# Pooled attention and feed-forward: two engines' queues in written order from chunk 3 on, attention in half-tile steps, and weight sums built in other buffers

## The chip, the cores and the metric

The kernel runs on one core of one Trainium2 chip. The metric is the device time of one execution in microseconds (us). TensorE (PE) multiplies, VectorE (DVE) and ScalarE (ACT) work on tiles in SBUF and PSUM, GpSimd (POOL) on tiles in SBUF alone, and SyncE (SP) issues most DMAs; a few DMAs are issued by ACT.

## The reference

```python
# q, k, v: [8 batches, 8 heads, 576, 64]; w_in: [512, 2048]; w_out: [2048, 512]; all float32
k_p = k.reshape(B, H, 72, 8, 64).mean(axis=3)          # keys and values pooled by 8
v_p = v.reshape(B, H, 72, 8, 64).mean(axis=3)
scores = q @ k_p.T / 8; scores -= max(scores)
attn = exp(scores); attn /= sum(attn) + 1e-9
x = heads_side_by_side(attn @ v_p)                       # 4608 tokens x 512
h = x @ w_in
out = maximum(0.01 * h, h) @ w_out                       # 4608 x 512
```

## The kernel before

The 4608 tokens are cut into nine chunks of 512, numbered 0 to 8. For each chunk the feed-forward multiplies on PE in split float32 (a high part and a low part of each operand), and beside it, in the same stretch of time, the attention of the next chunk's tokens is computed: `runs` lists the stretches, `beside` the attention pieces that go with each, and a stretch takes its attention steps one by one as its matmuls go by. The name of a chunk stands in its tiles' names: the tile B113xh is operand B11 of chunk 3, B116xh that of chunk 6. Chunks 3 to 8 use a scheme with seven products per quarter-block instead of eight (`pair`, `combine`, PE line 1080); it needs sums of weight blocks, which `prepare(j)` builds once for each of eight pairs of weight columns and ships to DRAM (`kept`), from where ACT's queue streams them in again for every chunk.

Batches 2 to 7 go through a path that transposes in DRAM. One half of a tile (four heads) takes these steps. PE computes scores (`s`, line 549), DVE the maximum, ACT four exponentials (559), DVE the reciprocal and POOL the normalised rows (`sb`, lines 593 and 599). SP writes them to DRAM (`rows`, line 606) and reads them back in another order (`blocks`, line 616). DVE transposes blocks of 32 (`pp`, line 628), ACT casts them to pT_hi (651), DVE makes pT_lo and the remainder (654, 658), all of which is the step `pu`. PE multiplies with the values (`au`, lines 673 to 676) and ACT copies the result into the next chunk's x (689). Keys and values of a batch are loaded by SP and summed by 8 on POOL in `lk` and `lv` (lines 264 and 271): k in two halves, its remainder, v in two halves, its remainder. The eight DMAs of v's remainder are at line 317. They all go through the pool tag `raw`, which has two buffers; tiles of the weight sums, and output tiles of one stretch (line 1212), have the same tag. `ku` places the keys (435, 440), and `vu` the values: v_hi on ACT (463), v_lo on DVE (466), v_parts on ACT (472), then four operations on DVE.

The order within an engine's queue comes from two sources. PE's instructions stand in written order (`manual_schedule`). On every other engine a planner orders them by a simulated timeline and by priorities, except for those marked with `keep_in_program_order`, which stay in written order among themselves. Each engine then runs its queue strictly in that order, so an instruction that waits holds up all behind it.

Of the kernel before, what the change touches and what calls it, by code (L numbers as in the profile page):

```python
# [24 lines left out]
def tile_pooled_attention_ffn(  # L25
# [52 lines left out]
    SUMS = ["S1", "S2", "S3", "S4", "A22"]  # L78
# [249 lines left out]
    def load_k(b):  # L328
        sums = one.tile([P, NK, D], F32, tag="ksum", name=f"ksum{b}") if b > 1 else addup[:, 7:]
        rem = k_rem  # L330
        if b < 2:
            rem = addup[:, 3 + 2 * b : 5 + 2 * b, :].unsqueeze(1)
        eng = nc.vector if b == 0 else nc.gpsimd
        raws = []

        def start():
            raws.extend(load_main(b, k, g, "k") for g in range(2))
            raws.append(load_k_rem(b))

# [22 lines left out]
        return start, finish  # L362

    def load_v(b):
# [25 lines left out]
        return start, finish  # L390

    tiles = [[x for piece in p for x in piece] for p in PIECES]
    every = [(b, t) for b in range(B) for t in range(len(tiles[b]))]

# [20 lines left out]
    def place_k(b, sums, rem):  # L415
# [11 lines left out]
        else:  # L427

            for i in range(2):
                for c in range(2):  # L430
                    to = slice(64 * i + 32 * c, 64 * i + 32 * c + 32)
                    cols = slice(32 * c, 32 * c + 32)
                    for x in range(2):
                        r = slice(64 * i + 32 * x, 64 * i + 32 * x + 32)
                        nc.vector.transpose(  # L435
                            kT[to, :, i, 32 * x : 32 * x + 32], sums[r, :, cols]
                        )
                    for x in range(2):
                        r = slice(32 * x, 32 * x + 32)
                        nc.vector.transpose(  # L440
                            kT[to, 2 * x : 2 * x + 2, :, MAIN:], rem[r, 0, i, cols]
                        )
# [7 lines left out]
    def place_v(b, sums, rem):  # L450
# [10 lines left out]
        for i in range(2):  # L461
            r = slice(64 * i, 64 * i + 64)
            nc.scalar.mul(v_hi[r, :, i, :], sums[r], 1.0 / POOL)
        for i in range(2):
            r = slice(64 * i, 64 * i + 64)
            nc.vector.scalar_tensor_tensor(
                v_lo[r, :, i, :], sums[r], 1.0 / POOL, v_hi[r, :, i, :].bitcast(F32),
                op0=ALU.mult, op1=ALU.subtract,
            )
        if b > 1:  # L470

            nc.scalar.mul(v_parts, rem, 1.0 / POOL)
            nc.vector.scalar_tensor_tensor(
                rem, rem, 1.0 / POOL, v_parts.bitcast(F32), op0=ALU.mult, op1=ALU.subtract
            )
# [31 lines left out]
    def q_unit(b, t, qr):  # L507
        n = tiles[b][t][1]
        if b > 1:
# [4 lines left out]
            nc.vector.transpose(  # L514
                qT[:, :, :n].rearrange("k p (s g) -> k g p s", g=m),
                blocks.rearrange("a (g p d) -> a g p d", g=m, p=NK),
            )
# [68 lines left out]
    def norm_via(b, t, g, e, sm):  # L586
# [16 lines left out]
        )  # L603
        rows = dram.tile([4, n, 96], F32, name=f"rows{b}_{t}_{g}")
        with tc.high_priority():
            nc.sync.dma_start(
                rows.rearrange("x a y -> a x y"), at[:n].rearrange("a x i j -> a x (i j)")
            )
        return rows

    def fetch_via(b, t, g, rows):

        m = tiles[b][t][1] // 32
        blocks = three.tile([P, 4, 3, 32], F32, tag="at", name=f"blocks{b}_{t}_{g}")
        with tc.high_priority():
            nc.sync.dma_start(
                blocks[:, :m].rearrange("p a i j -> p (a i j)"),
                rows.rearrange("x (s a) y -> (x s) (a y)", a=m),
            )
        return blocks  # L620

    def turn_via(b, t, g, blocks):
# [4 lines left out]
        tc.keep_in_program_order(  # L627
            nc.vector.transpose(  # L628
                pp[:, :, :n].rearrange("k i (s a) -> k a i s", a=m), blocks[:, :m]
            )  # L630
        )
# [137 lines left out]
    def attention(b):  # L769
# [5 lines left out]
        def loads():  # L775
            (start_k, st["k"]), (start_v, st["v"]) = load_k(b), load_v(b)
# [7 lines left out]
        def loads1():  # L784
            (start_k, st["k"]), (start_v, st["v"]) = load_k(b), load_v(b)
# [9 lines left out]
        def ku():  # L795
            place_k(b, *st["ks"])

        def vu():
            place_v(b, *st["vs"])

        def qu(t):
            def f():
                st["qT", t] = q_unit(b, t, q_of[b, t])
                after = every.index((b, t)) + 2
                if after < len(every) and every[after] not in q_of:
                    q_of[every[after]] = load_q(*every[after])
            return f

# [11 lines left out]
        def sb(t, g):  # L820
            def f():
                norm = norm_via if b >= VIA else norm_unit
                st["at", t, g] = norm(b, t, g, *st["e", t, g])
            return f

        def fe(t, g):
            def f():
                st["at", t, g] = fetch_via(b, t, g, st["at", t, g])
            return f

        def pu(t, g):
            def f():
                j, o = where[t]
                if (j, g) not in st:
                    st[j, g] = piece_tiles(b, j, g)
                p_unit(b, t, g, st["at", t, g], st[j, g], o)
            return f

        def au(j, g):
# [5 lines left out]
            "loads": loads1 if b else loads, "lk": lk, "lv": lv, "ku": ku, "vu": vu,  # L845
            **{f"q{t}": qu(t) for t in range(len(where))},
            **{f"s{t}": both(sa(t, 0), sa(t, 1)) for t in range(len(where))},
            **{f"{n}{t}{g}": u(t, g) for n, u in (("sa", sa), ("sb", sb), ("fe", fe), ("pu", pu))
# [61 lines left out]
    def line_up_via(pieces):  # L910

        flat = [(b, j, t) for b, j in pieces for t in range(len(tiles[b]))
                if tiles[b][t] in PIECES[b][j]]
        out, ends, free = [], {}, 0
# [20 lines left out]
        for n, (b, j, t) in enumerate(flat):  # L935
            nxt = flat[n + 1] if n + 1 < len(flat) else None
            if t == 0:
                out.append((b, "ku"))
            if n == 0:
                out.append((b, f"q{t}"))  # L940
            if nxt is None or nxt[:2] != (b, j):
                slots = stages(b, j, [x[2] for x in flat if x[:2] == (b, j)])
                if nxt and nxt[0] != b:
                    slots[-1].append((nxt[0], "vu"))
# [5 lines left out]
            for g in range(2):  # L950

                out.append(None if g else (b, f"s{t}"))
                if g == 0 and nxt:
                    out.append((nxt[0], f"q{nxt[2]}"))
                out.append((b, f"sb{t}{g}"))
                if g == 1 and n == 0 and t == 0:
                    out.append((b, "vu"))
                out += ends.pop(2 * n + g, [])
        for key in sorted(ends):
            out += [None, *ends[key]]  # L960
# [57 lines left out]

    kept = dram.tile([len(PAIRS), P, len(SUMS), 2, HALF], F32, name="kept")

    def prepare(j):

        ship = []
        f0, f1 = PAIRS[j]
        w = two.tile([P, 2, DM], F32, tag="raw", name=f"wsum{j}")
        for i, f in enumerate((f0, f1)):
            whole = ws[0, f].bitcast(F32)
            nc.gpsimd.tensor_tensor(w[:, i, :], whole[:, 0, :], whole[:, 1, :], op=ALU.add)
        (a11, a12), (a21, a22) = ((w[:, i, :HALF], w[:, i, HALF:]) for i in range(2))
# [4 lines left out]
        for i, names in enumerate((("S2", "S4"), ("S3", "S1"))):  # L1034
            both = two.tile([P, 2, DM], F32R, tag="raw", name=f"wsumhl{j}{i}")
            h, l = both[:, 0, :], both[:, 1, :]
            nc.scalar.copy(h, w[:, i, :])
            nc.gpsimd.tensor_tensor(l, w[:, i, :], h.bitcast(F32), op=ALU.subtract)
            for x, name in enumerate(names):
                ship.append((name, both.bitcast(F32)[:, :, x * HALF : (x + 1) * HALF]))  # L1040
        if j < OPEN:
            ship.append(("A22", ws[0, f1].bitcast(F32)[:, :, HALF:]))

        def send():
            for name, of in ship:
                tc.keep_in_program_order(nc.sync.dma_start(kept[j, :, SUMS.index(name)], of))
# [17 lines left out]
    def stream(eng, j, name):  # L1064

        if name == "S3":
            to, of = seat(name).bitcast(F32), kept[j, :, 2]
        else:
            seat(name)
            f, i, m = (2, 0, 2) if name == "S1" else (3, 3, 2 if j < OPEN else 1)  # L1070
# [212 lines left out]
    units = []  # L1283
    for n, pieces in enumerate(beside):
# [3 lines left out]
            for x in line_up_via([x for x in pieces if x[0] >= VIA])  # L1288
# [99 lines left out]
    going = list(range(len(PAIRS)))  # L1388
    for n in range(REST + FAST - 1, len(runs)):
# [4 lines left out]
        if nxt:  # L1394
            if nxt in waiting:
                us.insert(0, lambda nxt=nxt: carry(nxt))
            mid = len(us) // 2
            for b in early[n]:
                us[mid:mid] = [att[b]["lk"], att[b]["lv"]]
        beat = done = 0  # L1400
        for i, j in enumerate(going):
            final = i == len(going) - 1
            send()
            send = prepare(PREPARE[n, i]) if (n, i) in PREPARE else lambda: None
# [46 lines left out]
```

## Time and profile before

| what | value |
|---|---|
| three timed runs | 1007.02, 1004.08 and 1006.77 us, median 1006.77 us |
| profiled execution, its own time | 1004.5 us |
| its span, first to last instruction | 1002.7 us |
| mean granted TensorE clock | 0.959 of full speed |
| busy share of the span: PE, DVE, ACT, POOL | 90%, 53%, 48%, 30% |

The profiled execution's own time is the one that sums are made against; 1.8 us of it lie outside the span. A busy PE is not yet a PE at full speed, since it is counted as busy at half its clock too. The two levels of the clock are 2.4 and 1.2 GHz, so a granted clock of 0.94 over a stretch means that 12% of it ran at half speed.

### The profile page before, as it was taken

To read this page: it belongs to the slowest core of one execution; us is meant where nothing else is said; L and a number is where in the kernel's file an instruction comes from. 1 tells how busy PE (TensorE), PEld (TensorE's weight loads), DVE (VectorE), ACT (ScalarE), POOL (GpSimd) and SP (SyncE) were. 2 spreads that over 40 slices of the span, in tenths; PEclk is the share of its full clock that TensorE was granted. 3 is DMA by queue.
4 is the path that set the end of the run, shared out by engine and by line. 5 is a ranking of instruction groups with operands and counts; after the bars stand their busy time and mean duration, and the time that the engine had idled before them with its cause. 6 is when DMAs were issued, how large, how long until landed. Compare 5 with 4: busy or idle time off the path is not lost.

```text
span 1002.7 us, 15139 instructions
## 1 busy us (share of the span) xinstructions
PE 906.0 (90%) x5163; PEld 789.8 (79%) x5163; DVE 529.6 (53%) x1170; ACT 479.6 (48%) x1474; POOL 304.0 (30%) x470
## 2 busy tenths in 40 slices
PE   4689999979799779997899969997999899999998
PEld 4578898857688668886788858886988799988987
DVE  6998577543265444563555545654655453334212
ACT  6787576352254344453555425553555355344332
POOL 4501201735355764444333033411321022001000
PEclk9799999989799979999899979998999999999999
DMA  9963303354347513896178635863376316423432
GB/s 273 305 192 123 85 23 89 92 168 118 107 130 216 137 64 90 255 235 166 42 198 214 183 85 140 212 162 103 81 186 170 112 54 187 144 85 106 114 108 93
DMA packets 168717, 141.51 MB, mean 141 GB/s; under 512 B 101184, under 2 KB 141888, under 8 KB 168640
## 3 DMA queue, kind: packets, MB, share of 16 engines
q1 hardware_dynamic: 144976, 90.86, 33.2%
q10 hardware_dynamic: 23664, 49.68, 17.1%
q8 instruction: 41, 0.67, 0.3%
q14 instruction: 36, 0.29, 0.1%
HBM read 109.97 MB, written 30.54 MB: 140 GB/s over the span
## 4 chain that ended last, share of the span: by engine, by line
PE 38%; DMA 7%; DVE 4%; ACT 2%; POOL 2%; SPq 2%; issue 1%; ACTq 0%; POOLq 0%; DVEq 0%
PE ends_y L1080 10%; PE ends_x L1080 7%; PE acc L1174 6%; PE acc L1175 6%; PE acc L1176 6%; DMA vremraw<-in_v_dram 2%; PE pss L549 1%; DMA blocks<-rows 1%; DMA out_dram<-o 1%; DVE pp L628 1%; DVE kT L435 1%; PE pa L674 1%; DMA kremraw<-in_k_dram 1%; POOL vremraw L264 1%; PE pa L673 1%
## 5 line engine op out<-in xcount | busy, mean ns | idle before, releaser
L1174 PE MATMUL acc<-w,gh 128*128 128x512 f32 x576 | 232.1, 403 | 8.5 <-DVE o L1213 6.7
L1175 PE MATMUL acc<-w,gh 128*128 128x512 f32 x576 | 228.4, 397 | 0.0
L1176 PE MATMUL acc<-w,gl 128*128 128x512 f32 x576 | 226.6, 393 | 0.5 <-DVE gl L1111 0.5
L1174 PEld LDWEIGHTS acc<-w,gh 128*128 128x128 f32 x576 | 110.3, 192 | 25.5 <-issue 9.9
L1176 PEld LDWEIGHTS acc<-w,gl 128*128 128x128 f32 x576 | 109.4, 190 | 25.7 <-DVE gl L1111 0.9
L1175 PEld LDWEIGHTS acc<-w,gh 128*128 128x128 f32 x576 | 110.3, 191 | 14.0
L559 ACT ACTIVATE e<-pss,red 128x72 f32<-128x72 f32 (+1 forms) x320 | 97.9, 327 | 39.3 <-DVE red L557 36.6
L593 POOL TENSOR_TENSOR at<-e,red 128x128 f32<-128x128 f32 (+1 forms) x120 | 48.3, 422 | 149.0 <-DVE red L590 71.6
L992 PE MATMUL ph<-xh,w 128*128 128x512 f32 (+1 forms) x224 | 85.2, 380 | 0.4 <-DVE gl L1001 0.4
L993 PE MATMUL ph<-xl,w 128*128 128x512 f32 (+1 forms) x224 | 82.6, 369 | 0.0
L994 PE MATMUL ph<-xh,w 128*128 128x512 f32 (+1 forms) x224 | 82.5, 368 | 0.0
L673 PE MATMUL pa<-pT_hi,v_hi 128*128 128x256 f32 (+2 forms) x72 | 25.4, 353 | 47.6 <-ACT pT_hi L651 47.0
L559 ACT ACTIVATION_READ_ACCUMULATOR e<-pss,red 128x1 f32 (+1 forms) x320 | 68.1, 213 | 0.0
L651 ACT CAST pT_hi<-pp 128x384 fp32r<-128x384 f32 (+1 forms) x80 | 37.7, 474 | 49.8 <-DVE pp L628 46.2
L654 DVE TENSOR_TENSOR pT_lo<-pp,pT_hi 128x256 fp32r<-128x256 f32 (+1 forms) x80 | 38.2, 477 | 43.5 <-ACT pT_hi L651 43.2
L1001 DVE TENSOR_TENSOR gl<-ph,gh 128x512 fp32r<-128x512 f32 (+1 forms) x56 | 34.1, 610 | 48.3 <-ACT gh L1000 47.9
L1111 DVE TENSOR_TENSOR gl<-off,gh 128x512 fp32r<-128x512 f32 x48 | 34.2, 712 | 46.7 <-ACT gh L1110 46.2
L673 PEld LDWEIGHTS pa<-pT_hi,v_hi 128*128 128x128 f32 x72 | 15.8, 220 | 54.5 <-ACT pT_hi L651 52.7
L1139 ACT ACTIVATE dia<-dia 128x256 f32<-128x256 f32 x48 | 20.1, 419 | 74.8 <-DVE dia L1138 74.8
L1131 ACT ACTIVATE dia<-ends_x 128x256 f32<-128x256 f32 x48 | 18.6, 387 | 75.0 <-PE ends_x L1080 75.0
L628 DVE STREAM_TRANSPOSE pp<-blocks 128x384 f32<-128x384 f32 (+1 forms) x60 | 45.8, 763 | 16.2 <-DMA blocks<-rows 16.2
L1130 DVE TENSOR_TENSOR ends_y<-ends_y,dia 128x256 f32<-128x256 f32 x48 | 20.8, 434 | 60.3 <-PE ends_y L1080 60.2
(428 smaller groups left out, 2249.0 us busy)
## 6 DMA issues: line engine op xcount, KB each, us to landing
seat<-kept ACTq DMA_DIRECT2D x63, 512.0 KB
w<-kept ACTq DMA_DIRECT2D x42, 256.0 KB
rows<-at SPq DMA_DIRECT2D x48, 192.0 KB
blocks<-rows SPq DMA_DIRECT2D x48, 192.0 KB
out_dram<-o SPq DMA_DIRECT2D x34, 256.0 KB
w_bits<-in_moe_w_in_dram SPq DMA_DIRECT2D x16, 512.0 KB
w_bits<-in_moe_w_out_dram SPq DMA_DIRECT2D x16, 512.0 KB
kept<-wsumhl SPq DMA_DIRECT2D x32, 256.0 KB
```

The source lines that it names most:

```text
L559: ins = nc.scalar.activation(e[:n, h, :], scv[:n, h, :], AF.Exp, bias=mx[:n, h : h + 1], accum_out=sm[:n, h : h + 1],)
L593: nc.gpsimd.tensor_tensor(at[:n, :, i, :].rearrange("a (h f) j -> a h f j", h=2), e[:n, 2 * i : 2 * i + 2, 0:MAIN].rearrange("a h (f j) -> ...
L628: nc.vector.transpose(pp[:, :, :n].rearrange("k i (s a) -> k a i s", a=m), blocks[:, :m])
L654: nc.vector.tensor_tensor(pc["lo"][:, :, o : o + n], pp[:, 0:2, :n], pc["hi"][:, 0:2, o : o + n].bitcast(F32), op=ALU.subtract,)
L673: nc.tensor.matmul(pa, vh, pc["hi"][:, i, :w], start=True, stop=False)
L992: nc.tensor.matmul(ph, w[:, 0, ks], xh[kk][:, r], start=kk == 0, stop=False)
L993: nc.tensor.matmul(ph, w[:, 0, ks], xl[kk][:, r], start=False, stop=False)
L994: nc.tensor.matmul(ph, w[:, 1, ks], xh[kk][:, r], start=False, stop=kk == NK - 1)
L1080: nc.tensor.matmul(out, w[:, stay, ks], move, start=start and i + n == 0, stop=i + n == 3, skip_group_check=True,)
L1174: nc.tensor.matmul(a, gh[:, r], hi, start=first, stop=False)
L1175: nc.tensor.matmul(a, gh[:, r], lo, start=False, stop=False)
L1176: nc.tensor.matmul(a, gl[:, r], hi, start=False, stop=last)
```

## The change

- From the stretch of chunk 3 on, POOL's and SP's queues stand in written order as PE's does (`manual_schedule` over both), and a flag `pinned` is set. With it, `pin` marks operations on ACT and DVE to stay in written order among themselves: the scaling of k's sums, kT's transposes, v_hi, v_lo, v_parts and the first DVE step after it, q's and pp's transposes.
- From there on a new function `line_up_pinned` writes the attention's steps. The write of the normalised rows is a step of its own (`ro`), half a tile after `sb`; q's transpose and q's load are two steps; k's and v's loads and sums are seven steps `kv0` to `kv6`, each of which issues one load and sums the one before, spread over nine half tiles from the first tile of the batch before on; `ku` is four steps and `vu` three.
- In the stretches of chunks 0 (second half) and 2, `line_up_via` now writes a shorter sequence: `rows` follows `sb` and `blocks` comes just ahead of `pu`, without the raised priority that both had, and pp's transposes are not kept in order there.
- `prepare` builds the weight sums in buffers of x's high and low parts (tags xh0, xl0), free in the stretch of chunk 2, and no longer in `raw`. Four of its six additions go from POOL to DVE. All eight preparations stand in the stretch of chunk 2; before, two stood in chunk 0's second half, four in chunk 2 and two in chunk 3. What is shipped has the same size, in another arrangement of `kept`.

```diff
     def prepare(j):
...
-        w = two.tile([P, 2, DM], F32, tag="raw", name=f"wsum{j}")
...
+            return one.tile([P, DM], dtype, tag=f"x{part}0_{k}", name=f"{nm}{j}")
...
-        nc.gpsimd.tensor_tensor(a22, a21, a22, op=ALU.add)
-        nc.gpsimd.tensor_tensor(a21, a11, a21, op=ALU.subtract)
-        nc.gpsimd.tensor_tensor(a11, a22, a11, op=ALU.subtract)
-        nc.gpsimd.tensor_tensor(a12, a12, a11, op=ALU.subtract)
+        nc.vector.tensor_tensor(a22, a21, a22, op=ALU.add)
+        nc.vector.tensor_tensor(a21, a11, a21, op=ALU.subtract)
+        nc.vector.tensor_tensor(a11, a22, a11, op=ALU.subtract)
+        nc.vector.tensor_tensor(a12, a12, a11, op=ALU.subtract)
...
-    PREPARE = {
-        (4, 9): 0, (4, 12): 1, (5, 2): 2, (5, 5): 3, (5, 8): 4, (5, 11): 5, (6, 0): 6, (6, 2): 7,
-    }
+    PREPARE = {(REST + 1, f): j for j, f in enumerate((0, 2, 4, 6, 8, 10, 12, 13))}
...
+    def pin(ins):
+        return tc.keep_in_program_order(ins) if pinned else ins
...
-            nc.scalar.mul(v_parts, rem, 1.0 / POOL)
+            pin(nc.scalar.mul(v_parts, rem, 1.0 / POOL))
...
+    KV = {0: 1, 1: 2, 2: 3, 3: 4, 4: 5, 5: 6, 6: 8}
...
+    def line_up_pinned(pieces, ahead, fresh):
...
+            if t == 0 and b + 1 < B:
+                owed.extend([b + 1, i, after] for i, after in KV.items())
...
             for g in range(2):
+                if g == 0:
+                    out.append((b, f"s{t}"))
+                    if n:
+                        out.append((flat[n - 1][0], f"ro{flat[n - 1][2]}1"))
+                else:
+                    out.append((b, f"ro{t}0"))
+                    if nxt:
+                        out.append((nxt[0], f"qa{nxt[2]}"))
+                        if nxt[0] != b:
+                            out += [(nxt[0], f"ku{i}") for i in range(4)]
+                for x in owed:
+                    x[2] -= 1
+                out += [(x[0], f"kv{x[1]}") for x in owed if x[2] < 0]
...
+                out.append((b, f"sb{t}{g}"))
+                out += ends.pop(2 * n + g, [])
...
+    order.enter_context(tc.manual_schedule(engines={nc.gpsimd.engine, nc.sync.engine}))
+    pinned = True
     for n in range(REST + FAST - 1, len(runs)):
...
-            mid = len(us) // 2
-            for b in early[n]:
-                us[mid:mid] = [att[b]["lk"], att[b]["lv"]]
```

## Rows read from the trace of the kernel before

**Rows 1.** First products of chunks 3 to 7: duration min/median/max in ns, first and last start
```profile
L1080 PE MATMUL ends_x<-B113xh,w x32: 277/283/387, 387.1 to 485.7; 128*128 128x256 f32 x32
...
L1080 PE MATMUL ends_x<-B114xh,w x32: 277/283/415, 495.9 to 596.6; 128*128 128x256 f32 x32
...
L1080 PE MATMUL ends_x<-B115xh,w x32: 277/283/376, 606.8 to 703.3; 128*128 128x256 f32 x32
...
L1080 PE MATMUL ends_x<-B116xh,w x32: 277/283/375, 713.5 to 806.5; 128*128 128x256 f32 x32
...
L1080 PE MATMUL ends_x<-B117xh,w x32: 277/283/284, 816.6 to 898.6; 128*128 128x256 f32 x32
```
**Rows 2.** Windows by stretch: length, busy PE, PEld, DVE, ACT, POOL, granted clock, DMA
```profile
217.00:283.00 66.00, 52.27 (x220) 41.99 (x219) 23.12 (x46) 18.75 (x51) 26.21 (x35) 0.84 0.43 126
283.00:387.00 104.00, 91.14 (x399) 74.58 (x397) 53.52 (x104) 43.10 (x130) 69.89 (x88) 0.93 0.48 131
387.00:496.00 109.00, 95.44 (x594) 85.27 (x595) 55.53 (x117) 50.16 (x154) 44.60 (x61) 0.95 0.65 177
496.00:607.00 111.00, 100.20 (x604) 89.15 (x603) 59.81 (x135) 51.83 (x170) 33.48 (x56) 0.94 0.57 153
607.00:713.00 106.00, 96.60 (x598) 86.52 (x597) 57.44 (x134) 50.63 (x169) 30.36 (x53) 0.97 0.55 148
713.00:815.00 102.00, 96.32 (x596) 85.58 (x595) 55.34 (x131) 49.08 (x166) 18.96 (x36) 0.98 0.50 137
```
**Rows 3.** PE's waits from 387 to 906 us: total, times, longest
```profile
PE pa L673 <- ACT pT_hi L651: 29.0, 9, 8.3
PE ends_y L1080 <- ACT ends_y L1122: 6.0, 6, 1.7
```
**Rows 4.** The chain that ended last, between 462 and 482 us
```profile
466.52 7.10 DMA vremraw<-in_v_dram
...
473.92 1.27 POOL vremraw L264
```
**Rows 5.** ACT's timeline from 470 to 480 us, in brackets its idle time
```profile
477.72 0.31 ACT L472 ACTIVATE v_parts<-vremsum 128x128 fp32r<-128x128 f32 x1 [9.93 <-POOL vremsum L271]
477.93 0.49 ACT L651 CAST pT_hi<-pp 128x384 fp32r<-128x384 f32 x1
```
**Rows 6.** PE's waits from 190 to 387 us
```profile
PE pa L673 <- ACT pT_hi L651: 17.0, 4, 8.3
PE acc L1174 <- DVE o L1213: 6.7, 2, 5.3
```
**Rows 7.** ACT's timeline from 217 to 226 us
```profile
221.71 0.37 ACT L1212 COPY o<-acc 128x256 f32<-128x256 f32 x1 [1.37 <-POOL wsumhl L1038]
224.77 0.37 ACT L1212 COPY o<-acc 128x256 f32<-128x256 f32 x1 [2.69 <-DMA kept<-wsumhl]
```
**Rows 8.** ACT's timelines around 259 and around 352 us
```profile
259.14 0.62 ACT L1037 CAST wsumhl<-wsum 128x512 fp32r<-128x512 f32 x1 [6.02 <-POOL vremsum L271]
...
351.92 0.62 ACT L1037 CAST wsumhl<-wsum 128x512 fp32r<-128x512 f32 x1 [8.51 <-POOL vremsum L271]
```
**Rows 9.** Single lines: an addition on POOL, two operations on DVE, min/median/max in ns
```profile
L1030 POOL TENSOR_TENSOR wsum<-wsum x8: 723/734/742, 192.2 to 419.7; 128x256 f32<-128x256 f32 x8
...
L654 DVE TENSOR_TENSOR pT_lo<-pp,pT_hi x80: 253/425/1329, 23.5 to 893.7; 128x256 fp32r<-128x256 f32 x64, 128x128 fp32r<-128x128 f32 x16
...
L658 DVE SCALAR_TENSOR_TENSOR pT_hi<-pp,marks,pT_hi x80: 267/343/1462, 23.8 to 893.9; 128x128 fp32r<-128x128 f32 x64, 128x64 fp32r<-128x64 f32 x16
```
**Rows 10.** The way through DRAM: two chains, one wait, and v's remainder on SP
```profile
742.93 4.86 DMA rows<-at
...
640.87 5.52 DMA blocks<-rows
...
DVE pp L628 <- DMA blocks<-rows: 16.2, 5, 4.2
...
L317 SPq DMA_DIRECT2D vremraw<-in_v_dram x48: 619/624/707, 187.0 to 681.8; - x48
```

More of the change, by code (lines that the diff above doesn't have):

```diff
@@ L360, in finish, with piecewise, first, second @@
             return sums, rem
-        return start, finish
+        def piecewise():
+            def first():
+                raws.extend(load_main(b, k, g, "k") for g in range(2))
+            def second():
+                pooled(eng, sums[:, :2], raws[0], P)
+            def third():
+                raws.append(load_k_rem(b))
+                pooled(eng, sums[:, 2:], raws[1], P)
+                pin(nc.scalar.mul(sums, sums, KSCALE))
+            def fourth():
+                last = raws[2][:64, 0:1, 0:D]
+                pooled(eng, last, raws[2][:, 0:1, :], 64)
+                for i in range(2):
+                    eng.tensor_scalar(
+                        rem[:, 0, i, :], last[:, 0, :], sides[:64, i : i + 1], None, op0=ALU.mult
+                    )
+                return sums, rem
+            return first, second, third, fourth
+        return start, finish, piecewise
     def load_v(b):
@@ L614, in fetch_via @@
         blocks = three.tile([P, 4, 3, 32], F32, tag="at", name=f"blocks{b}_{t}_{g}")
[L615 to L619, printed above, removed]
+        nc.sync.dma_start(
+            blocks[:, :m].rearrange("p a i j -> p (a i j)"),
+            rows.rearrange("x (s a) y -> (x s) (a y)", a=m),
+        )
         return blocks
@@ L823, in f, with ro @@
                 st["at", t, g] = norm(b, t, g, *st["e", t, g])
+                if b >= VIA and not pinned:
+                    ro(t, g)()
+            return f
+        def ro(t, g):
+            def f():
+                st["at", t, g] = store_via(b, t, g, st["at", t, g])
             return f
@@ L935, in line_up_via @@
         for n, (b, j, t) in enumerate(flat):
[L936 to L940, printed above, removed]
+            nxt = flat[n + 1] if n + 1 < len(flat) else ahead
+            if n == 0 and fresh:
+                out.append((b, f"qa{t}"))
+            if t == 0 and b + 1 < B:
+                owed.extend([b + 1, i, after] for i, after in KV.items())
             if nxt is None or nxt[:2] != (b, j):
@@ L1017, in m2 @@
                 yield
-    kept = dram.tile([len(PAIRS), P, len(SUMS), 2, HALF], F32, name="kept")
+    kept = dram.tile([len(PAIRS), P, 5, 2, HALF], F32, name="kept")
     def prepare(j):
-        ship = []
-        f0, f1 = PAIRS[j]
-        w = two.tile([P, 2, DM], F32, tag="raw", name=f"wsum{j}")
[L1026 to L1029, printed above, removed]
-        nc.gpsimd.tensor_tensor(a22, a21, a22, op=ALU.add)
-        nc.gpsimd.tensor_tensor(a21, a11, a21, op=ALU.subtract)
-        nc.gpsimd.tensor_tensor(a11, a22, a11, op=ALU.subtract)
-        nc.gpsimd.tensor_tensor(a12, a12, a11, op=ALU.subtract)
[L1034 to L1040, printed above, removed]
@@ new lines, in row @@
+        def row(part, k, dtype, nm):
+            return one.tile([P, DM], dtype, tag=f"x{part}0_{k}", name=f"{nm}{j}")
+        f0, f1 = PAIRS[j]
+        w = [row("h", 2 * (j % 2) + i, F32, f"wsum{i}") for i in range(2)]
+        for x, f in zip(w, (f0, f1)):
+            whole = ws[0, f].bitcast(F32)
+            nc.gpsimd.tensor_tensor(x, whole[:, 0, :], whole[:, 1, :], op=ALU.add)
+        (a11, a12), (a21, a22) = ((x[:, :HALF], x[:, HALF:]) for x in w)
+        nc.vector.tensor_tensor(a22, a21, a22, op=ALU.add)
@@ L1283, in tile_pooled_attention_ffn, with line_of @@
     units = []
+    def line_of(n, pieces):
+        start = REST + FAST - 1
+        if n < start:
+            return line_up_via(pieces)
+        later = [x for x in beside[n + 1]] if n + 1 < len(beside) else []
+        ahead = None
+        if later:
+            b, j = later[0]
+            ahead = (b, j, tiles[b].index(PIECES[b][j][0]))
+        return line_up_pinned(pieces, ahead, n == start)
     for n, pieces in enumerate(beside):
@@ L1287, in tile_pooled_attention_ffn @@
             att[x[0]][x[1]] if x else lambda: None
-            for x in line_up_via([x for x in pieces if x[0] >= VIA])
+            for x in line_of(n, [x for x in pieces if x[0] >= VIA])
         ]
```

191 lines of the change are left out of this document (140 added, 51 removed).

## The prediction

> **What bounds the kernel now.** I read the stretches first. From chunk 3 on every stretch does the same feed-forward, so the distance between the first products of two chunks tells what the rest costs [rows 1]: 108.8 us from chunk 3 to 4 (495.9 - 387.1), then 110.9, 106.7 and 103.1. The windows show PE busy for nearly all of them, with a granted clock of 0.94 to 0.98 [rows 2]. So PE is the bound, and what can be won is of two kinds: its waits, and the time at half clock behind them, which is length times (1 - granted clock).
>
> PE's own waits come next. From 387 to 906 us the attention's last product waits for the cast of pT_hi for 29.0 us in nine waits, the longest of 8.3; copies on ACT cost another 6.0 [rows 3]. The clock adds 109 x 0.05 + 111 x 0.06 + 106 x 0.03 + 102 x 0.02 = 17.3 us [rows 2]. Together 52 us, the most that the ordered part of the kernel could give back.
>
> The chain of waits says why. Before PE's long wait near 470 us it goes through the DMAs of v's remainder (the last took 7.10 us) to POOL, which adds it up at 473.92 [rows 4]. ACT's timeline closes the circle: ACT stands idle for 9.93 us in front of v_parts, which needs that sum, and the cast of pT_hi, which PE wants, runs right behind it at 477.93 [rows 5]. v_parts belongs to the next batch, and nobody needs it then. The planner put it early since by its timeline the load had landed, and ACT's strict order made PE pay.
>
> In the earlier stretches the same happens with another instruction in front. ACT is held 6.02 us and 8.51 us at the cast of the weight sums, each time by POOL's sum of v's remainder [rows 8]; from 190 to 387 us PE waits 17.0 us for pT_hi, and 6.7 us at the turn to chunk 0's second half for an output copy [rows 6]. That copy waits for a buffer: ACT's two output copies are released by the weight sums and by their shipment [rows 7], and both use the tag raw.
>
> **The change part by part.** *k and v in seven steps, v_parts pinned behind v_hi.* v_hi may be overwritten only after the old batch's last `au`, so v_parts, now ordered behind it, can't get ahead of that batch's casts. The load itself moves forward: a batch's seven steps end about half a chunk before its `vu`. The stretch of chunk 6 is my measure for a stretch without this trouble: it has the same attention and feed-forward, and the last load of v's remainder starts at 681.8 [rows 10], before it begins. If chunks 3, 4 and 5 come to its 103.1 us, they give 5.7 + 7.8 + 3.6 = 17.1 us [rows 1]. Bounds: nothing, if another wait takes the place; 52 us if every wait and all half-clock time go. I take 17.1, since chunk 6 shows what is left of the waits with the loads gone, and its own last piece still waits.
>
> *Weight sums out of raw.* The wait for the output copy is priced at 6.7 us [rows 6] and, with half of that window's lost clock (66 x 0.16 = 10.6, shared with the next stall), 5.3 more: 12.0 us [rows 2]. But batch 3's k and v still use the same two buffers and may now move up into that place. From both sides, 0 and 12.0; I take half, 6.0.
>
> *No preparation in chunk 0's second half.* The cast that held ACT for 6.02 us there [rows 8] is gone; v_parts, unpinned in this stretch, stood next to it and can hold ACT in its stead. Price 6.0 + 5.3 = 11.3 us at most, nothing at least; half is 5.7.
>
> *All eight preparations in chunk 2.* Four more than before. POOL: an addition of 256 columns takes 0.734 us [rows 9], so one of 512 at most 1.47 as an estimate; a preparation falls from 8.8 to 5.9 us, and eight of the new in place of four old add 12 us to 69.9 of 104 [rows 2]. DVE: 32 additions at 0.425 us, the median of its nearest row [rows 9], are 13.6 us on top of 53.5 of 104. Both are hidden as long as PE has its matmuls; without that cover they would cost their 12 and 13.6 us. The danger is the order: each preparation now goes POOL, DVE, ACT, POOL, SP, and if POOL waits for v's remainder, DVE as well as ACT may stand. What PE loses in this stretch today is 17.0 - 6.0 + 104 x 0.07 = 18.3 us [rows 2, 6]. It may all go, since k and v no longer share buffers with the sums, or come twice. I take no change.
>
> One rule of the Trainium skill speaks against these additions. The row shows DVE operations with a median of 0.425 and 0.343 us that at times take 1.329 and 1.462 [rows 9]. The page "SBUF — State Buffer", section "SBUF: two separate sides", says that GpSimd and a DVE operation with two SBUF inputs share one port pair as an exclusive lock, whole instruction by whole instruction; that agrees with such a spread. By it each addition could cost up to its own 0.425 us and the wait for a POOL instruction; the rival below prices that from rows.
>
> *SP and POOL in written order.* PE's order is nearly what it was. What is queued behind a waiting SP instruction is now fixed: q's loads, k's and v's, `rows`, `blocks` and the stores stand in one line, and a `blocks` late by some us makes DVE wait at pp, which holds gl and with it PE. The way through DRAM takes 4.86 us for `rows` and 5.52 for `blocks` [rows 10], each with a half tile of its own now; some 100 us over a dozen such steps gives about 8 us each. That covers it, so I take nothing; if the cover fails it is the rival that makes the kernel slower. Shorter `line_up_via` in chunks 0 and 2: same DMAs, `au` half a tile sooner; inside the same two-sided bounds as the waits there.
>
> **The sum.** 17.1 + 6.0 + 5.7 = 28.8 us off the profiled execution's own 1004.5 us gives 975.7. The median of the runs shown is 2.3 us above that execution, so I predict 978 us.
>
> **The rivals.** *SP's line makes it slower.* Place: `blocks` in chunks 3 to 7, nine pieces of two halves, 18 fetches. For: pp already waits 16.2 us in five cases, 3.2 each [rows 10], and v's remainder alone occupies SP for 8 x 0.624 = 5.0 us. Against: the steps are spaced. If all 18 met such a 3.2 us wait and PE felt it, that is 58 us, and 1036 us; it decides from 28.8 / 18 = 1.6 us for each fetch on. At 2 us each: 978 + 36 = 1014 us. Chance 0.13.
>
> *Chunk 2 pays for the eight preparations.* Its stalls come twice: 978 + 18.3 = 996 us. For: ACT held 8.51 us there by the chain that now occurs twice as often [rows 8]. Against: the sums no longer take k's and v's buffers. Chance 0.17.
>
> *The early stalls go too.* The other halves and chunk 2's: 6.0 + 5.7 + 18.3 = 30.0 us more, 948 us. For: one cause, shared buffers and POOL's mixed queue. Against: those stretches stay with the planner, which misjudged the DMAs. Chance 0.10.
>
> *DVE waits for POOL at every addition.* 32 x (1.46 - 0.43) = 33 us more on DVE [rows 9], 100 of 104 us in that stretch: DVE would be level with PE, and half of it on the path gives 978 + 17 = 995 us. For: the long operations exist; against: the medians show them rare. Chance 0.05. This is what the Trainium skill's port rule would do here.
>
> *The stalls only change their names*, the planner placing other instructions too early: 1005 us, chance 0.06.
>
> The forecast keeps 0.49. Its own range, with the two halves at either end, is 966 to 990. For eight times in ten I go down to 957, which takes in part of the case of 948, and up to 1008, which takes in chunk 2, the port, no change and the mild end of SP's line: 957 to 1008. About 0.3% is what a measurement of this kernel can tell. Faster by more than that: 0.49 + 0.17 + 0.10 + 0.05 - 0.01 = 0.80; within: 0.07; slower: 0.13.
>
> **What would show it.** Right: ACT's idle time in front of v_parts gone; PE's wait for pT_hi after 387 us down from 29.0 to about a third; distances of first products near 103 us in chunks 3 to 5; no output copy released by the weight sums; the granted clock of those stretches up to 0.98. Wrong: pp waiting for `blocks` in many places, with SP idle at a store or a load in front of it; a longer chunk 2 with DVE or ACT held at the weight sums; PE waiting at the first products of chunk 3 because x's buffers still hold shipments.

## The result and the profile after

The changed kernel takes 958.1 us (median of four, 955.5 to 958.57), the kernel before 1005.42 us in the same runs: ratio 0.9524, 95% interval [0.9498, 0.955]. It is faster, by about 20 us more than the 978 us forecast: outside the forecast's own range of 966 to 990 us, and 1.1 us inside the wider one, which begins at 957. The profiled execution took 958.57 us itself (span 956.8), 45.9 us less than that of before.

The first products of chunks 3 to 7, which answer to [rows 1], place the gain:

```profile
L1233 PE MATMUL ends_x<-B113xh,w x32: 277/283/378, 369.5 to 456.2; 128*128 128x256 f32 x32
...
L1233 PE MATMUL ends_x<-B114xh,w x32: 277/283/283, 466.4 to 558.5; 128*128 128x256 f32 x32
...
L1233 PE MATMUL ends_x<-B115xh,w x32: 274/283/287, 568.7 to 659.7; 128*128 128x256 f32 x32
...
L1233 PE MATMUL ends_x<-B116xh,w x32: 277/283/287, 669.9 to 759.7; 128*128 128x256 f32 x32
...
L1233 PE MATMUL ends_x<-B117xh,w x32: 277/283/283, 769.9 to 851.8; 128*128 128x256 f32 x32
```

Chunk 3 starts 17.6 us earlier (369.5 for 387.1). The distances are 96.9, 102.3, 101.2 and 100.0 us where they were 108.8, 110.9, 106.7 and 103.1: 11.9, 8.6, 5.5 and 3.1 us less. Behind chunk 7's start some 0.8 us are lost. Together that is 45.9 us.

The windows of the same stretches, columns as in [rows 2]:

```profile
217.00:271.00 54.00, 47.42 (x224) 39.34 (x223) 32.12 (x55) 19.04 (x51) 31.04 (x37) 0.95 0.47 131
271.00:369.00 98.00, 88.12 (x397) 73.08 (x397) 63.01 (x120) 43.83 (x132) 57.40 (x71) 0.94 0.58 171
369.00:466.00 97.00, 94.35 (x594) 83.86 (x594) 55.53 (x114) 47.79 (x150) 29.86 (x47) 1.00 0.63 169
466.00:568.00 102.00, 96.65 (x601) 86.65 (x600) 62.63 (x136) 51.90 (x170) 32.76 (x55) 0.98 0.65 167
568.00:670.00 102.00, 97.99 (x606) 87.47 (x605) 61.47 (x136) 52.59 (x172) 35.38 (x57) 0.98 0.63 164
670.00:770.00 100.00, 96.96 (x603) 86.60 (x602) 58.29 (x135) 50.92 (x169) 21.98 (x40) 0.98 0.53 141
```

PE does the same matmuls with less half clock: 102 x 0.02 + 102 x 0.02 + 100 x 0.02 = 6.1 us in chunks 3 to 6 for 17.3 before. Its waits (total, times, longest), first from 190 to 370, then from 370 to 890 us, answer to [rows 6] and [rows 3]:

```profile
PE pa L724 <- DVE pT_lo L704: 7.4, 1, 7.4
PE ph L1140 <- DVE gl L1149: 6.3, 1, 6.3
PE pa L723 <- ACT pT_hi L701: 2.4, 2, 1.6
...
PE pa L723 <- ACT pT_hi L701: 9.3, 7, 2.3
```

From chunk 3 on the wait for the cast of pT_hi is 9.3 us for 29.0, about a third, as the prediction said it would be if right. What held it is gone, as ACT's and POOL's timelines show (to set beside [rows 4, 5]):

```profile
428.90 0.86 ACT L511 ACTIVATE v_hi<-vsum 64x256 fp32r<-64x256 f32 x2
...
431.53 0.30 ACT L520 ACTIVATE v_parts<-vremsum 128x128 fp32r<-128x128 f32 x1
...
467.13 0.79 POOL L270 TENSOR_TENSOR vremsum<-vremraw 128x128 f32<-128x128 f32 x1
```

v_parts stands behind v_hi with no idle time in brackets. POOL ends the remainder's sum for the batch after at 467.9 us; that batch's v_parts follows only at 537.3. Before, the corresponding wait ended at 477.7 with ACT standing in front of it.

Ahead of chunk 3 two long waits are left, both new: 6.3 us for gl and 7.4 us for pT_lo. The first ends at 269.7 us, at the turn to chunk 2. The preparations are written from chunk 2's first product on, one for every two weight columns, but in these stretches the planner orders POOL, and it runs the first ones closer together. POOL's timeline, then DVE's:

```profile
251.00 5.10 POOL L1178 TENSOR_TENSOR wsum<-w 128x512 f32<-128x512 f32 x4
...
261.20 2.89 POOL L1178 TENSOR_TENSOR wsum<-w 128x512 f32<-128x512 f32 x2
```
```profile
261.56 1.40 DVE L1183 TENSOR_TENSOR wsum<-wsum 128x256 f32<-128x256 f32 x1
262.88 1.50 DVE L1180 TENSOR_TENSOR wsum<-wsum 128x256 f32<-128x256 f32 x1
```

Each preparation begins with two additions on POOL (L1178). Of these 16, 7 run before the first output addition of the stretch of chunk 2 (DVE, 269.6 us), ahead of which two preparations at most are written. In the kernel before, 4 ran ahead of that point, 10 between it and chunk 3, and 2 in chunk 3. Of the chain that ended last between 255 and 270 us, 58% is the sums' additions on DVE. Beside POOL's additions one of them takes 1.40 or 1.50 us; at 259.14 us, with POOL idle, one takes 0.41.

DVE's and POOL's timelines around the second wait:

```profile
297.09 7.26 DVE L704 TENSOR_TENSOR pT_lo<-pp,pT_hi 128x128 fp32r<-128x128 f32 x1
...
296.98 0.44 POOL L648 TENSOR_TENSOR at<-e,red 128x128 f32<-128x128 f32 x1
297.39 1.26 POOL L1178 TENSOR_TENSOR wsum<-w 128x512 f32<-128x512 f32 x1
298.61 0.72 POOL L263 TENSOR_TENSOR v0raw<-v0raw 128x256 f32<-128x256 f32 x1
299.29 2.48 POOL L1188 TENSOR_TENSOR wsuml<-wsum,wsumh 128x512 fp32r<-128x512 f32 x2
301.73 2.48 POOL L1178 TENSOR_TENSOR wsum<-w 128x512 f32<-128x512 f32 x2
304.32 1.37 POOL L263 TENSOR_TENSOR v1raw<-v1raw 128x512 f32<-128x512 f32 x1
```

One DVE operation took 7.26 us, where the other fifteen of its size take 0.29 us on average. It lasts through six operations that POOL runs one behind the other, and ends at POOL's first pause, of 0.11 us.

### The profile page after: what moved, and what is told of

It is laid out like the page before. It is cut to its first block, busy times and chain, and to the rows that moved or that the text cites. A ratio compares the mean times of both kernels' runs of the same rounds, so it can differ in the third digit from the quotient of the medians.

```text
span 956.8 us, 15146 instructions
## 1 busy us (share of the span) xinstructions
PE 893.9 (93%) x5163; PEld 781.8 (82%) x5163; DVE 555.5 (58%) x1202; ACT 480.3 (50%) x1474; POOL 281.7 (29%) x438
## 4 chain that ended last, share of the span: by engine, by line
PE 71%; DVE 12%; DMA 5%; ACT 4%; SPq 3%; POOL 2%; issue 2%; ACTq 0%; POOLq 0%; DVEq 0%
PE ends_y L1233 13%; PE acc L1327 11%; PE acc L1328 11%; PE acc L1329 10%; PE ends_x L1233 9%; PE pss L598 3%; PE ph L1140 3%; PE ph L1142 3%; PE ph L1141 3%; DVE pT_lo L704 2%; DMA blocks<-rows 2%; DVE pp L679 1%; DMA kremraw<-in_k_dram 1%; PE pa L724 1%; ACT e L608 1%
## 5 line engine op out<-in xcount | busy, mean ns | idle before, releaser
L1327 PEld LDWEIGHTS acc<-w,gh 128*128 128x128 f32 x576 | 109.1, 189 | 15.4
L1328 PEld LDWEIGHTS acc<-w,gh 128*128 128x128 f32 x576 | 109.1, 189 | 14.0
L598 PE MATMUL pss<-kT,qT 128*128 128x144 f32 x320 | 50.6, 301 | 10.3 <-DVE kT L487 4.3
L598 PEld LDWEIGHTS pss<-kT,qT 128*128 128x128 f32 x320 | 46.2, 199 | 16.3 <-issue 7.5
L704 DVE TENSOR_TENSOR pT_lo<-pp,pT_hi 128x256 fp32r<-128x256 f32 (+1 forms) x80 | 42.9, 536 | 25.9 <-ACT pT_hi L701 25.6
L606 DVE TENSOR_REDUCE red<-pss 128x4 f32<-128x288 f32 (+1 forms) x80 | 35.8, 453 | 33.0 <-PE pss L598 31.2
L1140 PEld LDWEIGHTS ph<-xh,w 128*128 128x128 f32 x224 | 43.7, 195 | 13.1 <-DVE gl L1149 6.8
```

What stands on the lines that cost most here:

```text
L598: nc.tensor.matmul(sc[:, 2 * SP * i : 2 * SP * (i + 1)], qT[:, p, :], kT[:, p, :, :].rearrange("d i s -> d (i s)"), start=True, stop=True,)
L704: nc.vector.tensor_tensor(pc["lo"][:, :, o : o + n], pp[:, 0:2, :n], pc["hi"][:, 0:2, o : o + n].bitcast(F32), op=ALU.subtract,)
L1140: nc.tensor.matmul(ph, w[:, 0, ks], xh[kk][:, r], start=kk == 0, stop=False)
L1327: nc.tensor.matmul(a, gh[:, r], hi, start=first, stop=False)
L1328: nc.tensor.matmul(a, gh[:, r], lo, start=False, stop=False)
```

## The experiments

All lengths are of profiled executions: the start of chunk 3's first product, then its distance to chunk 4's, and so on.

| kernel | median us | ratio, 95% interval | chunk 3 starts | chunks 3, 4, 5, 6 |
|---|---|---|---|---|
| before | 1005.42 | | 387.1 | 108.8, 110.9, 106.7, 103.1 |
| changed | 958.1 | 0.9524 [0.9498, 0.955] | 369.5 | 96.9, 102.3, 101.2, 100.0 |
| e1_sums | 992.41 | 0.9849 [0.9805, 0.9892] | 382.7 | 96.9, 110.9, 106.6, 102.7 |
| e2_order | 962.45 | 0.9549 [0.9518, 0.958] | 372.4 | 98.2, 104.5, 99.7, 99.7 |
| e3_planner | 969.7 | 0.9609 [0.9566, 0.9651] | 364.6 | 101.2, 106.5, 106.1, 101.0 |
| e4_nopin | 953.64 | 0.9463 [0.9429, 0.9496] | 368.5 | 100.2, 101.0, 101.2, 97.8 |
| e5_lump | 996.76 | 0.9901 [0.9873, 0.9929] | 366.6 | 111.4, 113.9, 115.5, 101.7 |
| e6_poolsums | 952.66 | 0.946 [0.9399, 0.9521] | 363.7 | 97.7, 103.9, 99.6, 99.8 |
| e7_dvesums | 949.88 | 0.9435 [0.9385, 0.9485] | 361.6 | 97.2, 103.6, 101.4, 100.0 |
| e8_earlyline | 953.51 | 0.9472 [0.9421, 0.9522] | 365.4 | 97.0, 103.1, 100.0, 99.8 |
| e9_prio | 950.96 | 0.9472 [0.9452, 0.9492] | 364.8 | 97.4, 103.0, 99.8, 98.6 |
| e10_steps | 988.49 | 0.9827 [0.9783, 0.9871] | 372.5 | 100.9, 110.8, 108.0, 107.2 |
| e11_best | 942.47 | 0.9379 [0.9351, 0.9407] | 358.6 | 98.0, 102.5, 97.2, 97.8 |
| e12_pporder | 966.2 | 0.9602 [0.9568, 0.9636] | 379.7 | 97.6, 102.9, 99.5, 99.8 |

**The weight sums alone, and all but the weight sums.** To the kernel before came the new `prepare` with its places:

```diff
-    PREPARE = {
-        (4, 9): 0, (4, 12): 1, (5, 2): 2, (5, 5): 3, (5, 8): 4, (5, 11): 5, (6, 0): 6, (6, 2): 7,
-    }
+    PREPARE = {(REST + 1, f): j for j, f in enumerate((0, 2, 4, 6, 8, 10, 12, 13))}
...
-        w = two.tile([P, 2, DM], F32, tag="raw", name=f"wsum{j}")
+        w = [row("h", 2 * (j % 2) + i, F32, f"wsum{i}") for i in range(2)]
```

> The kernel before with the weight-sum part of the change alone (x's buffers, four additions on DVE, all eight preparations in chunk 2). Theory A, two separate gains: what was won ahead of chunk 3's first product (387.1 to 369.5 us) comes from the freed buffers, and the stalls at v_parts in chunks 4 and 5 stay: first product of chunk 3 near 370 us, chunks 4 and 5 still 111 and 107 us long, time 980 to 988 us. Theory B, one cause (the shared buffers alone): k and v load early enough, the stalls at v_parts go as well, time 960 to 968 us.

Measured 992.41 us, above the range of either theory; the lengths of the chunks are as theory A has them for 4 and 5. Chunk 3 is at once as short as in the changed kernel, and chunks 4 to 6 have not moved. In chunk 3 PE does not wait for pT_hi any more (8.3 us before), and the granted clock is 1.00 for 0.95. So for chunk 3 the weight sums' part is enough by itself. PE's waits of this kernel, first from 190 to 382, then from 382 to 900 us, still have the old cast:

```profile
PE pa L672 <- ACT pT_hi L650: 19.8, 4, 8.7
...
PE pa L672 <- ACT pT_hi L650: 20.6, 8, 7.7
```

The first output addition of the stretch of chunk 2 (DVE, 281.2 us before) starts at 270.7, 10.5 us earlier; from there to chunk 3 it takes 112.0 us where it took 105.9. With nothing else changed chunk 2 gets 6.1 us longer, though as many of the first additions run in it as before, 10 of 16. This is one execution, the fastest of four that range from 987.7 to 996.99 us.

The opposite kernel is the changed one with `prepare` as before, on POOL and in `raw`; only preparations 6 and 7 stand at the end of chunk 2 and not in chunk 3.

```diff
-            return one.tile([P, DM], dtype, tag=f"x{part}0_{k}", name=f"{nm}{j}")
+        w = two.tile([P, 2, DM], F32, tag="raw", name=f"wsum{j}")
...
+        (4, 9): 0, (4, 12): 1, (5, 2): 2, (5, 5): 3, (5, 8): 4, (5, 11): 5, (5, 12): 6, (5, 13): 7,
```

> The changed kernel with the weight sums as before: in raw's buffers, additions on POOL, the old arrangement in DRAM, preparations 0 to 5 at their old places and 6 and 7 at the end of chunk 2. Theory A: chunks 4 to 6 stay at 102, 101 and 100 us, and the start up to chunk 3's first product is at 385 to 395 us as before: time 974 to 984 us. Theory B: the gain in chunks 4 and 5 is lost too, time 995 to 1005 us.

Measured 962.45 us, better than either theory had it, with an interval that overlaps the changed kernel's. Its output addition starts at 270.3: what was won in chunk 0's second half is won here too, with two preparations in that half and in `raw`. Either part gives it, and the gains do not add; what in this part does it, no run tried by itself.

The same holds for chunk 3. The last two preparations run late, behind its first product at 372.4 us, as POOL's timeline shows; below it is SP's timeline of the kernel before:

```profile
373.53 2.52 POOL L1177 TENSOR_TENSOR wsum<-w 128x512 f32<-128x512 f32 x2
...
392.50 2.99 POOL L1177 TENSOR_TENSOR wsum<-w 128x512 f32<-128x512 f32 x2
```
```profile
429.09 6.07 SPq L1046 DMA_DIRECT2D kept<-wsumhl  x4
435.21 1.34 SPq L287 DMA_DIRECT2D k0raw<-in_k_dram  x2
```

With two preparations in the stretch chunk 3 takes 98.2 us, 10.6 less than before. So their work in the stretch does not cost those 11.9 us by itself. In the kernel before, the next batch's first load was issued right behind the last shipments, 48 us into chunk 3; here it is 37 us in, and with the weight sums alone it is ahead of chunk 3, at 342.9 us.

**Written order, marks, spacing.** Each edit is made on the changed kernel alone; the fourth takes the first two together.

```diff
-    order.enter_context(tc.manual_schedule(engines={nc.gpsimd.engine, nc.sync.engine}))
```

> The changed kernel without the written order on SP and POOL: the planner orders these two, the marks on ACT and DVE and the new steps stay. If the marks that hold v_parts behind v_hi do the work (theory A), chunks 3 to 6 lose at most 2 us each: 958 to 966 us. If the written order of the two queues does it (theory C), the stalls of chunks 3 to 5 return: 975 to 990 us.

```diff
     def pin(ins):
-        return tc.keep_in_program_order(ins) if pinned else ins
+        return ins
```

> The changed kernel with the marks on ACT and DVE taken off; SP and POOL stay in written order. Theory A: v_parts comes ahead of pT_hi's cast again and ACT idles at it in chunks 3 to 5, but its load now comes half a chunk earlier, so part of the 9.9 us waits returns: 965 to 980 us. Theory C: no change, 957 to 961 us.

```diff
-    KV = {0: 1, 1: 2, 2: 3, 3: 4, 4: 5, 5: 6, 6: 8}
+    KV = {i: 4 for i in range(7)}
```

> The changed kernel with all seven steps of k and v at one place, four half tiles after the first tile of the batch before, instead of one for each half tile. SP and POOL stand in written order, so SP waits for POOL's sums and POOL for SP's loads some 25 us in a row there, and the rows and blocks behind them are late. If the spacing of the seven steps is what the ordered queues need, chunks 3 to 5 get back their stalls: 975 to 1000 us. If it is enough that the loads come half a chunk ahead of their use, 957 to 965 us.

```diff
-        return tc.keep_in_program_order(ins) if pinned else ins
+        return ins
...
-    order.enter_context(tc.manual_schedule(engines={nc.gpsimd.engine, nc.sync.engine}))
```

> The changed kernel with neither the written order on SP and POOL nor the marks on ACT and DVE: only the steps are written as in the change (seven steps for k and v half a chunk ahead, rows half a tile after sb), the planner orders the rest. Without the written order alone it took 969.7 us, without the marks alone 953.6 us. If the place and spacing of the loads do most of the work (theory D), 962 to 975 us, and ACT's wait at v_parts costs PE nothing. If marks or written order are needed so that the planner does not undo the steps (theory A), 985 us or more.

Without the written order chunks 3 to 5 are 4.3, 4.2 and 4.9 us longer: 969.7 us, between the ranges of the two theories. Without the marks the time is 953.64, no worse than with them, and below both ranges expected. PE's waits of this run from 360 to 900 us, and the line of v_parts:

```profile
PE ends_y L1233 <- DVE dia L1291: 10.1, 9, 2.1
...
L520 ACT ACTIVATE v_parts<-vremsum x6: 310/310/346, 198.8 to 677.2; 128x128 fp32r<-128x128 f32 x6
```

The last v_parts again runs early for its batch, at 677.2 us for 737.2 in the changed kernel, but from 360 to 900 us ACT waits for v_parts once, for 1.2 us. So the mark on v_parts, on which the prediction built, is not what helps where SP and POOL stand in written order: the sum is there in time. Without marks and without written order the time is 988.49. Over the same stretch ACT then waits at v_parts three times, DVE waits 43.4 us at pp for the way through DRAM, and PE waits for DVE:

```profile
ACT v_parts L520 <- POOL vremsum L270: 12.7, 3, 5.8
...
DVE pp L679 <- DMA blocks<-rows: 43.4, 26, 5.5
...
PE ends_y L1233 <- DVE dia L1291: 21.1, 8, 3.9
```

So without the written order the marks are worth 18.8 us (988.49 - 969.7); which of them, no run shows.

With all seven steps in one place the time is 996.76, nearly the old one. SP's timeline, then DVE's and ACT's, and PE's waits from 360 to 900 us:

```profile
673.87 5.39 SPq L316 DMA_DIRECT2D vremraw<-in_v_dram  x8
679.37 0.86 SPq L668 DMA_DIRECT2D blocks<-rows  x2
...
685.35 0.87 DVE L679 STREAM_TRANSPOSE pp<-blocks 128x384 f32<-128x384 f32 x1 [5.91 <-DMA blocks<-rows]
...
686.30 0.51 ACT L701 CAST pT_hi<-pp 128x384 fp32r<-128x384 f32 x1 [7.21 <-DVE pp L679]
...
PE pa L723 <- ACT pT_hi L701: 24.2, 10, 8.1
```

`blocks` stands behind the eight DMAs of v's remainder; DVE, ACT and PE wait in turn, PE for 8.1 us. This is the rival of SP's line, and it is the spacing that keeps it away.

**DVE or POOL.** Four additions back to POOL, or the other way all sums on DVE:

```diff
-        nc.vector.tensor_tensor(a22, a21, a22, op=ALU.add)
+        nc.gpsimd.tensor_tensor(a22, a21, a22, op=ALU.add)
...
```

> The changed kernel with the four additions of each preparation back on POOL. If DVE's additions beside POOL's cost PE the wait of 6.34 us at 263 us, that wait goes and with it half-clock time, 948 to 955 us; POOL's runs get longer, so the 7.26 us operation on DVE may stay. If the additions on DVE pay as POOL's relief, the first product of chunk 3 comes later than 369.5 us and the time is 960 to 970 us.

```diff
-            nc.gpsimd.tensor_tensor(x, whole[:, 0, :], whole[:, 1, :], op=ALU.add)
+            nc.vector.tensor_tensor(x, whole[:, 0, :], whole[:, 1, :], op=ALU.add)
...
-            nc.gpsimd.tensor_tensor(l, x, h.bitcast(F32), op=ALU.subtract)
+            nc.vector.tensor_tensor(l, x, h.bitcast(F32), op=ALU.subtract)
```

> The changed kernel with all of the weight sums' additions and subtractions on DVE, none on POOL (ACT's casts stay). If DVE's 7.26 us operation and the lengthened additions come from POOL's two-input operations running at the same time, no DVE operation in chunk 2 is longer than 2 us, both waits of PE there (6.34 and 7.40 us) go with their half-clock time, and the time is 940 to 952 us. If DVE's own load is the limit (some 36 us of sums on top of 53 us in a stretch of 104), gl gets late and the time is 962 to 980 us.

On POOL 952.66 us, not told apart from the changed kernel. The wait for gl is down from 6.3 to 0.8 us; a long operation is still there, DVE's timeline shows it at another place:

```profile
283.20 3.31 DVE L638 TENSOR_TENSOR red<-red,tiny 128x4 f32<-128x4 f32 x1 [4.86 <-ACT e L608]
...
286.63 5.58 DVE L638 TENSOR_TENSOR red<-red,tiny 128x4 f32<-128x4 f32 x1
```

On DVE 949.88 us, and chunk 3 starts 7.9 us earlier than in the changed kernel. The 32 additions take 14.6 us, where beside POOL's sums they took 21.8. No DVE operation takes more than 1.8 us, but this alone shows nothing of POOL: e1_sums, e3_planner, e4_nopin, e5_lump and e8_earlyline have the sums split as in the changed kernel, and in none of them does one take more than 1.82. Two gaps of PE of about 4 us stay.

**What moved the early stretches.** Three edits, each on top of the one before: the old `line_up_via` for the early stretches, the raised priority of `rows` and `blocks` there, and pp's transposes kept in program order there.

```diff
-                later(n + 1, 0, [(b, f"pu{x}0") for x in mine])
+                slots = stages(b, j, [x[2] for x in flat if x[:2] == (b, j)])
...
```

> The changed kernel with the longer sequence of steps of before in the stretches of chunk 0's second half and chunk 2 (blocks read in steps of their own, au half a tile later). The run with the weight sums alone came to chunk 3's first product at 382.7 us, the one with everything else at 372.4 us, so if the shorter sequence is the cause of that, the first product goes back to 380 to 385 us and the time is 969 to 975 us. If something else moved there with it (the priority of rows and blocks, the planner's view of what follows), 957 to 962 us.

```diff
-        nc.sync.dma_start(
+        with nullcontext() if pinned else tc.high_priority():
+            nc.sync.dma_start(
...
```

> The run with before's steps in the early stretches, and on top of it the raised priority that rows and blocks had there. Sums alone came to chunk 3's first product at 382.7 us, this base at 365.4 us, with the same steps and the same sums. If the planner's raised priority is what made the difference (rows and blocks pushed ahead of the loads and shipments on SP), the first product goes to 378 to 385 us and the time to 966 to 972 us. If it is pp's fixed order or the planner's view of what follows, the first product stays at 363 to 368 us and the time at 951 to 956 us.

```diff
-        pin(nc.vector.transpose(
+        tc.keep_in_program_order(nc.vector.transpose(
             pp[:, :, :n].rearrange("k i (s a) -> k a i s", a=m), blocks[:, :m]
```

> The changed kernel with the earlier sequence of steps and the raised priority of rows and blocks in the stretches without an order by hand (as in the run with raised priority), and besides with the transposes into pp kept in the order of the program on DVE there too. With that, the early stretches differ from the kernel with the weight sums' part alone only in k's and v's loads of the batches behind and in what the planner sees of the rest. If the fixed place of these transposes is what cost the kernel before its time ahead of chunk 3, chunk 3's first product starts at 378 to 385 us and the time is 966 to 970. If the cause lies in the rest of the kernel, as the planner sees it, the first product stays at 363 to 367 us and the time near 951. From chunk 3 on nothing differs, so the lengths of the chunks stay within 1.5 us of 97.4, 103.0, 99.8, 98.6 and 92.1 either way.

The first two give 953.51 us (below both ranges expected) and 950.96, no slower than the changed kernel, and chunk 3 starts 4 to 5 us earlier: neither the shorter sequence nor the lower priority is the cause of the gain. The third gives 966.2 us; chunk 3 starts at 379.7 for 364.8, and the chunks behind it stay within 1.2 us. ACT's timeline with pp's order kept, then DVE's further on, and last ACT's without that order:

```profile
250.47 0.31 ACT L520 ACTIVATE v_parts<-vremsum 128x128 fp32r<-128x128 f32 x1 [7.02 <-POOL vremsum L270]
250.69 0.49 ACT L703 CAST pT_hi<-pp 128x384 fp32r<-128x384 f32 x1
...
340.75 1.48 DVE L1200 TENSOR_TENSOR wsum<-wsum 128x256 f32<-128x256 f32 x1
342.26 1.37 DVE L1201 TENSOR_TENSOR wsum<-wsum,wsum 128x256 f32<-128x256 f32 x1
343.67 0.43 DVE L1202 TENSOR_TENSOR wsum<-wsum,wsum 128x256 f32<-128x256 f32 x1
344.13 0.43 DVE L1203 TENSOR_TENSOR wsum<-wsum 128x256 f32<-128x256 f32 x1
...
345.07 1.13 DVE L681 STREAM_TRANSPOSE pp<-blocks 128x192 f32<-128x192 f32 x2
```
```profile
242.14 0.55 ACT L703 CAST pT_hi<-pp 128x384 fp32r<-128x384 f32 x1
250.54 0.31 ACT L520 ACTIVATE v_parts<-vremsum 128x128 fp32r<-128x128 f32 x1 [7.85 <-POOL vremsum L270]
```

v_parts holds ACT for 7 to 8 us either way. With pp's order kept, the cast of pT_hi comes behind it (PE waits 5.5 us), and later pp behind four additions (PE waits 7.8 us); without it the cast is through at 242.7 and nobody whom PE needs stands behind v_parts. Why the planner puts the casts there when pp is fixed, no run shows.

**A version that beats both.** All sums on DVE, no marks, and the old early sequence.

```diff
-        return tc.keep_in_program_order(ins) if pinned else ins
+        return ins
...
-            nc.gpsimd.tensor_tensor(x, whole[:, 0, :], whole[:, 1, :], op=ALU.add)
+            nc.vector.tensor_tensor(x, whole[:, 0, :], whole[:, 1, :], op=ALU.add)
...
```

> The three single edits that were each faster than the changed kernel, together: all weight sums on DVE (949.9 us), no marks on ACT and DVE (953.6), before's steps in the early stretches (953.5). If they act in different places, their gains of 8, 4.5 and 4.6 us add up: 940 to 945 us. If the first and the last take away the same stalls in chunk 2, 945 to 950 us.

942.47 us. Its windows of chunk 0's second half and chunk 2 (columns as above) show the clock up and POOL relieved:

```profile
217.00:271.00 54.00, 50.79 (x244) 42.12 (x243) 32.88 (x78) 19.50 (x63) 17.25 (x26) 1.00 0.45 127
271.00:358.00 87.00, 81.48 (x373) 67.39 (x372) 64.61 (x132) 42.65 (x121) 32.27 (x49) 0.98 0.67 194
```

## Why the prediction was right, and where it was not

The time came inside the range, but the sum held 28.8 us and 45.9 came off the profiled execution: 12.0 more in chunks 3 to 6 and 6.0 more in chunk 2, less 0.9 elsewhere.

*k and v in seven steps, 17.1 us.* The term was too small, because chunk 6's 103.1 us is no floor. Chunk 3 came to 96.9, chunks 4 and 5 to 102.3 and 101.2, and chunk 6 itself to 100.0, where PE's waits fell from 5.7 to 2.9 us. Together they gave 29.1 us. Chunks 4 to 6, which the weight sums alone do not move, gave 8.6 + 5.5 + 3.1 = 17.2 of it. That this equals the forecast is luck: the forecast had 5.7 of its 17.1 in chunk 3 and nothing in chunk 6. The circle of [rows 4, 5] was read rightly, and the signs named for it came: no idle time ahead of v_parts from chunk 3 on, the wait down to 9.3 us, the clock at 0.98. The means was wrong. With SP and POOL in written order, the marks, that behind v_hi among them, do nothing measurable; the load half a chunk ahead does, and it needs the spacing and one of written order and marks.

*The weight sums' effect on chunk 3, not in the sum.* This is the step that failed. The prediction priced the weight sums ahead of chunk 3 alone and not in the stretch that they leave. By itself the part shortens chunk 3 by 11.9 us (108.8 to 96.9), of which the sum held 5.7 under another name. The rest of the change without it gives 10.6, so either part cuts the circle there. Which of the sums' own steps does it, the freed buffers or the new places, no run separates.

*Chunk 0's second half, 6.0 + 5.7 = 11.7 us.* Right in total, by luck: 281.2 to 269.6 is 11.6, but each term was half of a bound, and the weight sums alone give 10.5, the rest without them 10.9. It is one gain that either part brings, and not two halves. The ground of the second term did not come about: 7 of the 16 first additions run ahead of that point, and ACT still stands 9.0 us in three waits at the cast of the weight sums (L1187, 256.9 to 263.0 us). v_parts holds it besides, for 8.07 us at 251.1 us, as that term feared.

*Chunk 2, no change.* From the output addition to chunk 3 it takes 99.9 us for 105.9. The weight sums alone make it 6.1 us longer, about a third of the rival's 18.3. POOL's busy time there was to rise by 12 us and fell from 69.9 to 57.4: 9 of the 16 first additions run in it and not all, and before it was 10 and not 8. The gain is from pp's transposes, named in the change beside the shorter sequence and not priced: letting them go takes 108.5 to 97.7, and 4.1 us in the half before. [rows 6] put 17.0 us of waiting on pT_hi from 190 to 387 us; with pp's order put back it is 17.7. Of the rival that the early stalls go too, this is the part that came true.

*Written order, nothing.* Right as to its danger: the cover of half a tile holds, DVE's wait at pp after 360 us falls from 10.4 to 1.0 us, and without the spacing it fails as the rival said. The rival's 18 fetches were miscounted: from 387 us on SP issues 44 (L616), so it would have decided from 28.8 / 44 = 0.7 us for each. Wrong as to its worth: left out, it costs 11.6 us (969.7 - 958.1), though about 5 us are made up in front of chunk 3.

*DVE waiting for POOL.* The rival's place was right and its form wrong. The 32 additions take 21.8 us for the 13.6 forecast, 0.68 each and not 1.46. Besides, single operations are held far longer, and one of 7.26 us cost PE 7.4 us. The Trainium skill, "SBUF — State Buffer", section "SBUF: two separate sides", says that of a GpSimd operation and a DVE operation with two SBUF inputs, whichever starts first gets the shared pair of ports for that whole instruction. The additions of 1.40 and 1.50 us agree with that: neither is longer than one of POOL's (1.29) and its own 0.41 together. But 7.26 us spans six POOL instructions of 0.72 to 1.3 us, so DVE's turn did not come after one of them; why, no run shows.

## What to carry to other kernels

When work is moved from one stretch to another, price the stretch that it leaves as carefully as the one where it arrives, and see in the trace where the planner put it. A circle of waits over two strict queues can be cut at several places, so the gains of parts that touch it do not add, and the cut that counts may be a small mark, such as one operation's fixed order. In a hand-written queue the spacing of the bulk transfers is what keeps the short, urgent ones on time.

## What was unexpected of the hardware

A DVE operation with two operands in SBUF stood through a whole run of POOL operations: 7.26 us for one whose fellows take 0.29, and 5.58 us for one on four elements per partition. Such holds are rare. In most runs with the same sums on POOL no DVE operation took more than 1.82 us, so what starts a long one is open, and that POOL's work is what holds it was argued from the timelines. What the runs do show is the smaller effect: with all of the sums on DVE its 32 additions take 14.6 us, beside POOL's sums 21.8.
